# A planned one-core kernel (spectral filter, gated with a state-space scan): angle rounding in one ScalarE operation, four skip products on VectorE, single chunks at the end, joined products

## The chip, the cores and the metric

One core of one Trainium2 chip runs the whole kernel in one launch. Its engines work beside each other: TensorE (PE, matmuls into PSUM; its weight loads are a row of their own, PEld), VectorE (DVE), ScalarE (ACT), GpSimd (POOL, here almost only as issuer of accumulating transfers) and SyncE (SP, issuer of nearly all other transfers). The metric is the device time of one execution in microseconds; lower is better. Most executions of one kernel agree within 0.3%.

## What is computed

The input x has 2048 rows (sequence) and 1024 columns. Two branches are computed from it and mixed by a gate with one value per row:

```
x = A_x                                          # 1 x 2048 x 1024, bf16
g = sigmoid((x * gate_w).sum(-1, keepdims=True))
a = irfft2(rfft2(x) * (w_r + 1j * w_i))          # over rows and columns

dt = exp(log_dt); Lam_bar = exp(dt * Lam)        # 1024 complex states
Bu = x @ (((Lam_bar - 1) / Lam)[:, None] * B).T
h[t] = Lam_bar * h[t - 1] + Bu[t]                # 2048 steps
b = 2 * Re(h @ C.T) + x * Dskip
return g * a + (1 - g) * b
```

Both branches are given the same x.

## The kernel before, in words

**Spectral branch.** Both Fourier transforms are matmuls with constant cosine and sine tables. The row transform is split in two stages (16 x 128). Per step of 16: forward column transform (`fd`, L640), first row stage (`s1`, L663), a turn through DRAM, second row stage with the product by W on VectorE (`s2w`, L751; the product is L765, one operation for each of the two parts of W), first inverse stage (`is1`, L772), another turn through DRAM, second inverse stage and inverse column transform (`is2` L788, `idft` L804). Each result is moved out of PSUM by ScalarE. `idft` scales by the gate (L817) and writes half-folded rows to DRAM; `unfold` (L905) reads them back for two row tiles and adds and subtracts (L913, L917) into a buffer `ga`.

**State-space branch.** States are handled in eight blocks of 128 (`jb`), rows in four chunks of 512 (`c`). For a block, `bu` (L860) computes B x in PSUM (L870, 16 matmuls of 512 columns for a chunk), ScalarE moves it to `h` (L873), `rot` (L831) turns it by an angle that grows with the row, so that the scan on VectorE (L882) is a real one with one factor per state, and `rot_out` (L849) turns it back. A rotation is two products (L838, L839) and two sums (L840 and L842 or L844). It takes one chunk (n=1) or two (n=2). Before the change `bu` takes two chunks in each turn; `rot_out` takes chunks 0 and 1 singly and chunks 2 and 3 together. Blocks 6 and 7 come in the order (6, first half), (7, first half), (6, second half), (7, second half).

**Tables.** `table` (L610) makes cosine and sine for a block: the angle in turns is `tau * theta`; its nearest whole number is found by adding a large constant (L617, ScalarE, out in fp32) and taking it off again (L619, ScalarE), VectorE subtracts it (L620), ScalarE takes the sine of both parts (L622 to L624), casts them to bf16 singly (L625, L626), and scaled copies (L627, L628) feed the products with the input coefficients (L629, L632).

**Gates.** `gates` (L581): 32 matmuls with one output row each, sigmoid (L594), a cast to fp32 for each of four rows (L597), and a turn through DRAM into two layouts, `gA` (for L817) and `gB` (for 1 - g, `omg`).

**Output.** `yout` (L921), one row tile `tb` of 128 of the 16: 64 matmuls `h` x `C` of 512 columns (L929), in four groups `pc` of two state blocks, then the skip `x * Dskip` as eight matmuls of 128 columns with a diagonal matrix (L936). For tiles 0 to 11 ScalarE scales the result by 1 - g into two halves `y32` (L944), GpSimd issues transfers that add them onto `ga` (L945), and `ga` goes out (L947). For tiles 12 to 15 VectorE does it in one operation (L952) and SP sends `o` (L955); tile 15 in two halves.

**What sets the order.** Nothing is written in order of time. Each operation is entered in a `Plan` (L168) with an engine, a key, an assumed duration, and what it reads and writes. `Plan.run` (L236) goes through them once while the kernel is built: it takes the engine that can start soonest, and on it, among those that can start then, the operation with the lowest key. That fixes the order on every engine. The keys are linear in the block or tile number with the constants `K_...` (L386 to L428). Buffers are given from groups with few slots: four of PSUM (`ps`), two for `ga` and the transposed B (`bt`), eight in `cs` for tables, `y32` and `o`, five in `e4` for the unfold.

## Time and profile before

| what | us |
|---|---|
| median of 3 executions (lowest, highest) | 324.64 (324.59, 326.59) |
| the profiled execution, its own time | 325.01 |
| its span, first to last instruction | 323.2 |
| TensorE busy | 308.9 (96%) |
| VectorE busy | 285.2 (88%) |
| ScalarE busy | 204.6 (63%) |
| GpSimd busy | 22.5 (7%) |

All numbers of lines and groups are those of the profiled execution, whose time lies 1.81 us over its span. A row of a group of instructions reads: line, engine, operation, output and inputs, shapes, count, then busy time in us and mean ns of one, then the idle time of its engine just before and what ended it. Matmuls are pipelined, so the mean of one (379 ns at 512 columns) is longer than the spacing of two; spacings are read from the chain of work that ended last, whose pieces follow each other without gaps. The mean granted TensorE clock is 0.999.

### The profile page before, as it was taken

Reading aid. Unit: us, or ns where it says so; the run is one execution under the profiler, and the core shown is the slowest. Engines: PE = TensorE matmul, PEld = TensorE weight load, DVE = VectorE, ACT = ScalarE, POOL = GpSimd, SP = SyncE. Lnnn points to the kernel's source line nnn. Section 1 sums busy time; section 2 is a strip of 40 time slices with the busy share of each in tenths; the row PEclk is TensorE's granted clock in tenths of the full one; section 3 lists DMA queues with packets and bytes.
Section 4 is the critical chain, followed back from the end, with each engine's and each line's share of the span. In section 5 each row is a group of like instructions: output and inputs, shape, how many; then the busy total and the mean of one; then the engine's idle time right before and its main releaser. Section 6 shows DMA issues by size and latency. Waiting matters only on the chain.

```text
span 323.2 us, 5180 instructions
## 1 busy us (share of the span) xinstructions
PE 308.9 (96%) x1869; PEld 165.3 (51%) x1869; DVE 285.2 (88%) x448; ACT 204.6 (63%) x280; POOL 22.5 (7%) x32
## 2 busy tenths in 40 slices
PE   5988999999999999999988999999999999999994
PEld 4753666654444444444556655544544444454452
DVE  3999999999999999999899999999999999931114
ACT  3799999999899998999999998301411110050000
POOL 1000000000000000000000000000420242162000
PEclk9999999999999999999999999999999999999999
DMA  7996247795979999995699997970750368977003
GB/s 228 390 231 4 65 145 210 147 268 150 284 172 302 260 258 259 224 267 83 160 262 250 267 256 220 198 256 2 120 108 2 76 121 171 187 102 128 32 3 127
DMA packets 79408, 56.50 MB, mean 175 GB/s; under 512 B 49684, under 2 KB 65428, under 8 KB 79384
## 3 DMA queue, kind: packets, MB, share of 16 engines
q1 hardware_dynamic: 75848, 53.03, 63.5%
q0 software_dynamic: 3456, 3.15, 9.2%
q8 instruction: 14, 0.23, 0.3%
q14 instruction: 10, 0.08, 0.1%
q10 hardware_dynamic: 80, 0.01, 0.0%
HBM read 28.38 MB, written 16.79 MB: 140 GB/s over the span
## 4 chain that ended last, share of the span: by engine, by line
PE 62%; ACT 17%; DMA 9%; DVE 6%; issue 3%; SPq 2%; DVEq 0%; ACTq 0%
PE ps_y L929 34%; PE psu L870 14%; PE ps_id L812 2%; DMA wA<-in_A_w_r_dram 2%; PE ps_y L936 2%; ACT h L782 2%; ACT M_all L801 2%; PE ps_fd L648 2%; PE ps_fd L653 2%; PE ps_s L668 2%; DVE wA L765 1%; ACT h L873 1%; DMA Bcol<-turn_scratch 1%; DMA wB<-in_A_w_i_dram 1%; DMA xn<-in_A_x_dram 1%
## 5 line engine op out<-in xcount | busy, mean ns | idle before, releaser
L870 PE MATMUL psu<-xT,BTs 128*128 128x512 bf16 x512 | 116.7, 379 | 2.5 <-ACT M_all L513 1.1
L929 PE MATMUL ps_y<-CT,h 128*128 128x512 bf16 x512 | 113.6, 379 | 0.0
L870 PEld LDWEIGHTS <-BTs 128*128 128x128 bf16 x512 | 49.6, 98 | 61.0 <-issue 4.2
L929 PEld LDWEIGHTS <-h 128*128 128x128 bf16 x512 | 49.4, 98 | 56.0
L882 DVE TENSOR_TENSOR_SCAN h<-r_sb,carry,h 128x512 bf16<-128x512 f32 x48 | 60.0, 1272 | 0.0
L944 ACT ACTIVATE y<-ps_y,omg 128x512 f32<-128x512 f32 x24 | 15.3, 684 | 70.5 <-PE ps_y L936 60.8
L945 POOL DMA_DIRECT2D ga<-y x24 | 21.2, 1170 | 269.5 <-DVE h L840 225.5
L873 ACT CAST h<-psu 128x1024 bf16<-128x1024 f32 x32 | 32.4, 1022 | 3.0 <-PE psu L870 3.0
L840 DVE TENSOR_TENSOR h<-h,su 128x1024 bf16<-128x1024 bf16 (+1 forms) x40 | 23.0, 574 | 0.2
L839 DVE TENSOR_TENSOR h<-h,pn 128x1024 bf16<-128x1024 bf16 (+1 forms) x24 | 20.7, 861 | 0.1
L838 DVE TENSOR_TENSOR su<-h,pn 128x1024 bf16<-128x1024 bf16 (+1 forms) x24 | 20.6, 858 | 0.0
L839 DVE TENSOR_TENSOR h<-h,cs 128x2048 bf16<-128x2048 bf16 x16 | 19.5, 1221 | 0.2
L838 DVE TENSOR_TENSOR su<-h,cs 128x2048 bf16<-128x2048 bf16 x16 | 19.3, 1205 | 0.0
L882 DVE TENSOR_TENSOR_SCAN h<-r_sb,h 128x512 bf16<-128x512 f32 x16 | 18.8, 1208 | 0.0
L952 DVE SCALAR_TENSOR_TENSOR o<-ps_y,omg,ga 128x1024 bf16<-128x1024 f32 (+1 forms) x5 | 5.3, 1069 | 12.8 <-issue 11.0
L782 ACT CAST h<-ps_is 128x1024 bf16<-128x1024 f32 x16 | 16.0, 1017 | 0.4 <-PE ps_is L779 0.4
L917 DVE TENSOR_TENSOR ga<-G_all 128x512 bf16<-128x512 bf16 x16 | 5.9, 417 | 11.4 <-DMA out_dram<-ga 11.4
L762 ACT CAST h<-ps_s 128x1024 bf16<-128x1024 f32 x16 | 15.8, 1021 | 0.0
L478 PE MATMUL pt<-ident,xn 128*128 128x128 bf16 x128 | 10.1, 242 | 5.1 <-DMA xn<-in_A_x_dram 3.8
L817 ACT ACTIVATE M_all<-ps_id,gA 128x1024 bf16<-128x1024 f32 x12 | 13.6, 1162 | 1.0 <-PE ps_id L812 1.0
L801 ACT CAST M_all<-ps_is 128x1024 bf16<-128x1024 f32 x12 | 12.6, 1060 | 1.3 <-PE ps_is L797 1.3
L812 PE MATMUL ps_id<-G_all,M_all 128*128 128x256 bf16 x96 | 12.4, 273 | 0.8 <-ACT M_all L801 0.8
(135 smaller groups left out, 406.2 us busy)
## 6 DMA issues: line engine op xcount, KB each, us to landing
xn<-in_A_x_dram SPq DMA_DIRECT2D x16, 256.0 KB
h<-turn_scratch SPq DMA_DIRECT2D x16, 256.0 KB
turn_scratch<-h SPq DMA_DIRECT2D x16, 256.0 KB
M_all<-turn_scratch SPq DMA_DIRECT2D x13, 256.0 KB
ga_scratch<-M_all SPq DMA_DIRECT2D x12, 256.0 KB
M_all<-ga_scratch SPq DMA_DIRECT2D x6, 512.0 KB
ga<-y POOLq DMA_DIRECT2D x24, 128.0 KB, 5.0
out_dram<-ga SPq DMA_DIRECT2D x12, 256.0 KB
```

Of the source, the lines that this page charges most:

```text
L762: act(key, 1.01, lambda: nc.scalar.copy(out=X2.t, in_=ps2.t), r=[(ps2,)], w=[(X2,)])
L782: act(key, 1.01, lambda: nc.scalar.copy(out=C1.t, in_=psc.t), r=[(psc,)], w=[(C1,)])
L801: act(key, 1.01, lambda: nc.scalar.copy(out=ZT.t, in_=psz.t), r=[(psz,)], w=[(ZT,)])
L812: mm(pz.t[:, at, :], lhsT=ZT.t[:, 2 * par + half, c, :], rhs=Gi_sb[:, par, half, c, :], start=(half == 0), stop=(half == 1))
L838: dve(key, w, lambda: nc.vector.tensor_mul(out=sv(), in0=src()[:, ::-1], in1=bc(1)), r=sitem + [titem(1)], w=[(su,)])
L839: dve(key, w, lambda: nc.vector.tensor_mul(out=dst(), in0=src(), in1=bc(0)), r=sitem + [titem(0)], w=ditem)
L840: dve(key, h, lambda: nc.vector.tensor_add(out=dst()[:, 0], in0=dst()[:, 0], in1=sv()[:, 0]), r=[(su,)] + r0, w=r0)
L870: mm(psu.t[:, ri, :], lhsT=BT.t[:, ri, db, :], rhs=xT[c][:, db, :], start=(db == 0), stop=(db == 7))
L873: act(kb[cc] + K_KA, 1.01, lambda cc=cc, psu=psu: nc.scalar.copy(out=g()[:, :, cc, :], in_=psu.t), r=[(psu, 0), (psu, 1)], w=ui(cc) + ([(" ...
L882: dve(kd, 1.25, lambda cc=cc, ri=ri, carry=carry: nc.vector.tensor_tensor_scan(out=g()[:, ri, cc, :], data0=rb, data1=g()[:, ri, cc, :], i ...
L929: mm(psy.t[:, 512 * dh:512 * (dh + 1)], lhsT=hbuf[jb // 4].t[:, jb % 4, ri, P * tb:P * (tb + 1)], rhs=CT[pc].t[:, ri, jb % 2, 512 * dh:512 ...
L945: dma(key - 1, 1.3, lambda cols=cols, y32=y32: nc.gpsimd.dma_start(out=ga.t[:, tb % 2, cols], in_=y32.t, accum_op=ALU.add), r=[(y32,)] + [ ...
```

## The change

- `table`: L617 writes its product with `theta` straight as int32 (which rounds it), L619 is left out, the subtraction reads int32. The two casts to bf16 become one of both halves.
- `gates`: the rows stay bf16 on the way through DRAM; the four casts are left out, and one small ScalarE copy makes `gA` fp32.
- `s2w`: one VectorE product over both parts of W in place of two.
- `bu` takes a first chunk and a count. The second half of blocks 6 and 7 goes chunk by chunk, in the order (6, chunk 2), (7, chunk 2), (6, chunk 3), (7, chunk 3).
- `rot_out`: chunks 0 and 1 of blocks 0 to 5 together; those of blocks 6 and 7 singly as before; chunks 2 and 3 of these two singly.
- `yout`: tiles 12 to 15 have no skip matmuls. VectorE multiplies the tile's rows of x by a row of Dskip that was spread over the partitions by a transfer, and sums (1 - g) times that and `ga` into a new fp32 buffer `ro`; the last operation adds `ro`. Tile 15 is made and sent in pieces of 512, 256 and 256 columns. x, Dskip's row and `ro` take slots of the groups `cs` (up to four) and `e4` (up to four).
- All `K_...` constants have other values, and there are four new ones.

The diff, cut to its core:

```diff
-    g_dram = dram.tile([S], FP32, name="g_scratch")
+    g_dram = dram.tile([S], BF16, name="g_scratch")
...
-                 "Cq": ("m", 3), "ZT": ("m", 2), "eo": ("m", 3), "eoc": ("e4", 3), "pq": ("e4", 2)})
+                 "Cq": ("m", 3), "ZT": ("m", 2), "eo": ("m", 3), "eoc": ("e4", 3), "pq": ("e4", 2), "xs": ("cs", 4), "ro": ("e4", 4)})
...
-    K_UN = 3245.96
+    K_UN = 2287.79
-    K_R1 = -842.33
-    K_R2 = 2615.95
-    K_RS = 140.01
+    K_R1 = 1065.73
+    K_R2 = 5537.31
+    K_RS = 84.32
-    K_Y = -5745.79
-    K_YS = 508.42
+    K_Y = -5275.43
+    K_YS = 317.37
+    K_R3 = 1947.99
+    K_R4 = -1072.73
+    K_D3 = 1520.12
+    K_SK = -886.66
...
-        act(key, 0.72, lambda: A2(out=kk(), in_=tau_f, func=ACT.Identity, scale=at(thn), bias=MAGIC),
-            r=[("tau",), ("tht0",)], w=[(tt, 0)])
-        act(key, 0.63, lambda: A2(out=kk(), in_=kk(), func=ACT.Identity, bias=-MAGIC), r=[(tt, 0)], w=[(tt, 0)])
-        dve(key, 0.75, lambda: nc.vector.scalar_tensor_tensor(out=rr(), in0=tau_f, scalar=at(thn), in1=kk(), op0=ALU.mult,
+        act(key, 0.72, lambda: A2(out=kk().bitcast(I32), in_=tau_f, func=ACT.Copy, scale=at(thn)), r=[("tau",), ("tht0",)], w=[(tt, 0)])
+        dve(key, 0.75, lambda: nc.vector.scalar_tensor_tensor(out=rr(), in0=tau_f, scalar=at(thn), in1=kk().bitcast(I32), op0=ALU.mult,
...
-        act(key, 0.62, lambda: nc.scalar.copy(out=cs.t[:, 1, :], in_=sn_f()), r=[(tf, 0)], w=[(cs, 1)])
-        act(key, 0.62, lambda: nc.scalar.copy(out=cs.t[:, 0, :], in_=cs_f()), r=[(tf, 1)], w=[(cs, 0)])
+        act(key, 1.04, lambda: nc.scalar.copy(out=cs.t, in_=tf.t), r=[(tf, 0), (tf, 1)], w=[(cs, 0), (cs, 1)])
...
-            act(key, 0.6, lambda rr=rr: nc.scalar.copy(out=grow_f.t[rr, :], in_=grow.t[rr, :]), r=[(grow, c)], w=[(grow_f, c)])
...
+        act(key + 20, 0.22, lambda: nc.scalar.copy(out=gA, in_=gA_bf), r=[("gA_bf",)], w=[("gA",)])
...
-        for i in range(2):
-            dve(key + K_WD, 0.69, lambda i=i: nc.vector.tensor_mul(out=Z(b, i), in0=X2.t, in1=Z(b, i)),
-                r=[(X2,)], w=[wr + (i, c, o) for c, o in parts])
+        dve(key + K_WD, 1.22, lambda: nc.vector.tensor_mul(out=Zs(b), in0=X2.t[:, None, :, :].to_broadcast([P, 2, 2, K]), in1=Zs(b)),
+            r=[(X2,)], w=[wr + (i, c, o) for i in range(2) for c, o in parts])
...
+    dsk = tile_of([P, D], BF16, "dsk", "xs")
+    dma(K_UN - K_DM, 0.9, lambda: nc.sync.dma_start(out=dsk.t, in_=B_Dskip.rearrange("(o d) -> o d", o=1).to_broadcast([P, D])), r=[("step", 15, 1)], w=[(dsk,)])
...
-        order = [(pc, dh) for pc in range(4) for dh in range(2)] if tb < 15 else [(pc, dh) for dh in range(2) for pc in range(4)]
+        parts = [(0, 512), (512, 1024)] if tb < 15 else [(0, 512), (512, 768), (768, 1024)]
+        order = [(pc, v) for pc in range(4) for v in parts] if tb < 15 else [(pc, v) for v in parts for pc in range(4)]
...
+        if tb >= SKIP:
+            xs = tile_of([P, D], BF16, "xs", "xs")
+            dma(key - K_DM, 0.85, lambda: nc.sync.dma_start(out=xs.t, in_=x[P * tb:P * (tb + 1), :]), r=[("step", 15, 1)], w=[(xs,)])
+            ro = tile_of([P, D], FP32, "ro", "ro")
+            dve(key + K_SK, 0.69, lambda: nc.vector.tensor_mul(out=xs.t, in0=xs.t, in1=dsk.t), r=[(xs,), (dsk,)], w=[(xs,)])
+            dve(key + K_SK, 1.27, lambda: nc.vector.scalar_tensor_tensor(out=ro.t, in0=xs.t, scalar=og, in1=ga.t[:, tb % 2], op0=ALU.mult, op1=ALU.add),
+                r=[(xs,), ("omg",)] + ri_[0] + ri_[1], w=[(ro,)])
...
-    KD = lambda p: KB(p, 0) + K_D + K_KR * p + K_D1 * turns[p][1]
+    KD = lambda p, c0: KB(p, 0) + K_D + K_KR * p + K_D1 * (c0 > 0)
...
-    turns = [(jb, pr) for jb in range(6) for pr in range(2)] + [(6, 0), (7, 0), (6, 1), (7, 1)]
+    turns = [(jb, c0, 2, 2 * jb + c0 // 2) for jb in range(6) for c0 in (0, 2)]
+    turns += [(6, 0, 2, 12), (7, 0, 2, 13), (6, 2, 1, 14), (7, 2, 1, 14.5), (6, 3, 1, 15), (7, 3, 1, 15.5)]
...
+            if c0 == 0:
+                if jb < 6:
+                    rot_out(jb, 0, 2, KD(p, 0) + K_O)
+                else:
+                    rot_out(jb, 0, 1, KD(p, 0) + K_O)
+                    rot_out(jb, 1, 1, K_R1 + K_RS * jb)
             else:
-                rot_out(jb, 2, 2, K_R2 + K_RS * jb)
+                rot_out(jb, c0, n, (K_R2, K_R3)[c0 == 3] + K_RS * jb + K_R4 * (n == 1))
```

More of the change, by code (lines that the diff above doesn't have):

```diff
@@ L347, in tile_of @@
         if group == "e4":
-            return plan.buf(tag, lambda i: view(G_all[:, 2048 * (4 - i):2048 * (5 - i)] if i >= 3 else M_all[:, 2048 * i:2048 * (i + 1)], shape))
+            return plan.buf(tag, lambda i: view(G_all[:, 2048 * (4 - i):2048 * (5 - i)] if i >= 3 else M_all[:, 2048 * i:2048 * (i + 1)], shape, dtype))
         if group == "f":
@@ L575 @@
     sv(5, lambda: V.tensor_scalar_mul(out=ns2[:, :, 0], in0=sTC, scalar1=-1.0), ["sn2"], ["ns2a"])
-    gB, gA, omg = [cpool.tile([P, 16], FP32, name=n) for n in ("gB", "gA", "omg")]
-    omg_bf = cpool.tile([P, 16], BF16, name="omg_bf")
+    gA, omg = [cpool.tile([P, 16], FP32, name=n) for n in ("gA", "omg")]
+    gB, gA_bf, omg_bf = [cpool.tile([P, 16], BF16, name=n) for n in ("gB", "gA_bf", "omg_bf")]
     def gates(key):
@@ L943, in yout @@
                 y32 = tile_of([P, K], FP32, "y32", "cs")
-                act(key - 1, 0.72, lambda cols=cols, y32=y32: A2(out=y32.t, in_=psy.t[:, cols], func=ACT.Copy, scale=og), r=[(psy, dh), ("omg",)], w=[(y32,)])
+                act(key - 1, 0.72, lambda cols=cols, y32=y32: A2(out=y32.t, in_=psy.t[:, cols], func=ACT.Copy, scale=og), r=[(psy, 512 * dh), ("omg",)], w=[(y32,)])
                 dma(key - 1, 1.3, lambda cols=cols, y32=y32: nc.gpsimd.dma_start(out=ga.t[:, tb % 2, cols], in_=y32.t, accum_op=ALU.add),
```

148 lines of the change are left out of this document (76 added, 72 removed).

## The prediction, written before the result

> **What bounds the kernel now.** I read the page first: busy time and the 40 slices.
>
> ```profile
> PE 308.9 (96%) x1869; PEld 165.3 (51%) x1869; DVE 285.2 (88%) x448; ACT 204.6 (63%) x280; POOL 22.5 (7%) x32
> PE   5988999999999999999988999999999999999994
> DVE  3999999999999999999899999999999999931114
> ACT  3799999999899998999999998301411110050000
> ```
>
> TensorE is nearly always busy, VectorE until about 285 us, ScalarE until about 200 us. Averages hide which of them starves the others, so next came the windows of 20 us and TensorE's waits.
>
> ```profile
> 20.00:40.00 20.00, 18.87 (x101) 10.11 (x100) 19.74 (x29) 18.81 (x27) 0.00 (x0) 1.00 0.56 77
> 160.00:180.00 20.00, 18.10 (x162) 12.56 (x159) 19.97 (x33) 19.98 (x24) 0.00 (x0) 1.00 0.99 236
> 180.00:200.00 20.00, 19.22 (x147) 12.00 (x145) 19.86 (x30) 18.88 (x26) 0.00 (x0) 1.00 1.04 265
> 200.00:220.00 20.00, 20.00 (x112) 10.17 (x109) 19.98 (x33) 4.15 (x4) 0.00 (x0) 1.00 0.70 197
> 280.00:300.00 20.00, 20.00 (x118) 10.02 (x117) 6.17 (x14) 5.06 (x8) 6.99 (x8) 1.00 0.73 134
> ```
>
> ```profile
> PE psu L870 <- ACT M_all L513: 1.1, 1, 1.1
> PE ps_id L812 <- ACT G_all L801: 0.9, 2, 0.6
> PE ps_id L812 <- ACT M_all L801: 0.8, 1, 0.8
> PE psu L870 <- ACT G_all L817: 0.6, 1, 0.6
> PE psu L870 <- ACT M_all L817: 0.4, 1, 0.4
> ```
>
> The columns of a window are its length, then busy time of PE, weight loads, VectorE, ScalarE and GpSimd, the clock, the DMA share. From 200 us TensorE has no hole; the clock is 1.00. Its holes are: the first load of x, which nothing in the change touches, 1.1 us near 25 us, and 1.90 + 0.78 = 2.68 us between 160 and 200, where each wait is for a ScalarE eviction and ScalarE is busy 19.98 of 20. So time comes off in three places only: TensorE's own work, its waits for ScalarE, and what follows the last matmul. VectorE at 19.9 of 20 is busy beside TensorE, but TensorE does not wait for it.
>
> **The skip product leaves TensorE.** The chain at the end:
>
> ```profile
> 314.49 0.45 PE ps_y L936 x8
> 314.94 1.73 PE ps_y L929 x8
> 316.67 0.46 PE ps_y L936 x8
> 317.21 1.28 DVE o L952
> 318.53 0.75 DVE o L952
> 319.28 0.66 DVEq L1046
> ```
>
> ```profile
> 317.81 0.61 PE L936 MATMUL ps_y<-diag,xT 128*128 128x128 bf16 x8
> 47.97 0.44 PE ps_fd L648 x4
> ```
>
> Four tiles lose eight L936 matmuls each: 4 x 0.45 = 1.80 us, in a stretch where TensorE never waits. Tile 15's second half in two quarters turns 16 matmuls of 512 columns (1.73 / 8 = 0.216) into 32 of 256 (0.44 / 4 = 0.110): +0.06. Sum **-1.74**. A matmul of 128 columns costs 0.45 / 8 = 0.056 us here. The Trainium skill, page "TensorE: Matmul & The Clock Gate", section "Back-to-back issue gap", gives some 81 ns as the sustained spacing at 128 columns and 56 ns for an isolated one; by the 81 the 32 matmuls would be worth 2.6 us, an estimate from that page. The trace has 0.056 in a stream with weight loads, so I keep the row.
>
> **The end.** Tile 14's last matmul ends at 317.13; VectorE then adds tile 14 (1.28) and tile 15's halves and is done at 319.28 + 0.66 = 319.94; TensorE ends at 317.81 + 0.61 = 318.42, so 1.52 us of VectorE follow it, and 323.2 - 319.94 = 3.26 us of output DMA. New: after tile 14 TensorE has 0.86 (512 columns, one pc), 0.44 (256, one pc) and 0.88 (256, two) = 2.18 us left. VectorE's 1.28 covers the first; the pieces cost 0.75, 0.48 and 0.48 (1283 - 747 = 536 ns for 512 columns less, so 747 - 268), done 3.1 to 3.2 us after tile 14, some 1.0 behind TensorE in place of 1.52. **-0.5**. The last DMA has half the bytes; I count nothing for that (between 0 and -0.3, a tenth of its 3.26).
>
> **What VectorE gets in exchange, and the joins.**
>
> ```profile
> L838 DVE TENSOR_TENSOR su<-h,cs 128x2048 bf16<-128x2048 bf16 x16 | 19.3, 1205 | 0.0
> L840 DVE TENSOR_TENSOR h<-h,su 128x1024 bf16<-128x1024 bf16 x24 | 16.4, 684 | 0.2
> L840 DVE TENSOR_TENSOR h<-h,su 128x512 bf16<-128x512 bf16 x16 | 6.6, 410 | 0.0
> L765 DVE TENSOR_TENSOR wA<-h,wA 128x1024 bf16<-128x1024 bf16 x16 | 10.3, 689 | 0.1
> L952 DVE SCALAR_TENSOR_TENSOR o<-ps_y,omg,ga 128x1024 bf16<-128x1024 f32 x3 | 3.9, 1283 | 12.7 <-issue 11.0 <-PE ps_y L936 1.8
> L952 DVE SCALAR_TENSOR_TENSOR o<-ps_y,omg,ga 128x512 bf16<-128x512 f32 x2 | 1.4, 747 | 0.0
> ```
>
> Added: 4 x (0.69 + 1.28) = 7.9 us, the product by the 1024-wide row of L765, the fused sum by that of L952. W multiply joined: 16 x (1.21 - 2 x 0.689) = -2.7. Output rotation joined for chunks 0 and 1 of blocks 0 to 5: 2 x (2 x 0.69 + 2 x 0.41) = 4.4 becomes 2 x 1.21 + 2 x 0.68 = 3.8, six times: -3.6. The last two blocks' second half chunk by chunk: the same 0.6 back for two rotations in two blocks: +2.4. Net +4.0. It costs TensorE nothing: the sums need ga of tiles 12 to 15, so they fall into 285 to 312 us, where VectorE is idle (6.17 busy of 20 from 280 on; the 11.0 idle ahead of L952). The products can run earlier, in the full stretch, for 2.8 us, against 3.6 + 2.7 - 2.4 = 3.9 saved there. If that cover went, the next thing late would be tiles 8 to 11's last quarter at 282. The loads are 4 x 256 KB of x and 256 KB of Dskip on SP's queue, 1.25 of 56.5 MB, while the DMA engines are half empty; the Dskip load has no writer to wait for and can go out early, and x follows the last inverse step near 204 us, 90 us before its use.
>
> **What ScalarE loses.**
>
> ```profile
> L617 ACT ACTIVATE tt<-tau_f,tht 128x512 f32<-128x512 f32 x8 | 6.0, 746 | 0.5 <-DVE tht L550 0.5
> L619 ACT ACTIVATE tt<-tt 128x512 f32<-128x512 f32 x8 | 5.2, 649 | 0.1
> L625 ACT CAST cs<-tf 128x512 bf16<-128x512 f32 x8 | 5.1, 643 | 0.0
> L597 ACT CAST M_all<-M_all 1x512 f32<-1x512 bf16 x4 | 2.5, 616 | 0.1
> L467 DVE CAST tau_f<-tau_i 128x512 f32<-128x512 int32 x1 | 0.4, 426 | 0.0
> ```
>
> Per table: L619 goes (0.65), two copies of 0.64 become one of about 1.04: 0.9, eight times 7.1 us. Gates: four copies of 0.62 go, one small one (0.2) comes: 2.3. Together -9.4 of 204.6. The first operation of a table keeps L617's price, with int32 out; the VectorE operation that reads int32 is not in the trace, but L467 reads int32 at 0.43 us for 512, so I expect no loss; were it twice its 0.74, 6 us over eight tables would fall on VectorE, covered as above. Head: the table of block 0 stands in ScalarE's queue ahead of the eviction for which TensorE waits 1.1 us; L619 gone is 0.5 to 0.6 of it, I take **-0.4** (bounds: -1.1, the whole wait, and +0.5, another operation put there). 160 to 200 us: relief there is 2.3 of the gates just before it and 0.9 of the last table, 3.2 us, against 2.68 of waits. Not each eviction wait ends by relief elsewhere, and every priority is new. I take three quarters, **-2.0** (bounds: -2.7, and +1.9, a second hole like the worst window's).
>
> **Sum.** 323.2 - 1.74 - 0.5 - 0.4 - 2.0 = 318.56 us span; with the 325.01 - 323.2 = 1.81 around it, 320.4 for an execution like the profiled one. That one lies 0.37 over the median of 324.64, so the forecast is **320.0**, -1.4%.
>
> **Rivals.**
> First, only what leaves TensorE counts: the new priorities fill the ScalarE stretch otherwise and the holes stay. 323.2 - 2.24 = 320.96, **322.4** as a median. For it: ScalarE still stands at 195 of 323 us, nearly all before 200, so it stays as full there as the order lets it. Against: it is the releaser of every hole, and it has less to do.
> Second, all holes close: -1.74 - 0.5 - 1.1 - 2.7 - 0.3 gives 316.9, **318.3** as a median. Against: the plan balances three full engines.
> Third, slower: the slots for the scaled tiles run out.
>
> ```profile
> L944 ACT ACTIVATE y<-ps_y,omg 128x512 f32<-128x512 f32 x24 | 15.3, 684 | 70.5 <-PE ps_y L936 60.8 <-issue 6.1 <-DMA ga<-y 2.6
> 245.75 6.91 PE ps_y L929 x32
> 282.58 1.26 ACT L944 ACTIVATE y<-ps_y,omg 128x512 f32<-128x512 f32 x2 [20.82 <-PE ps_y L936]
> 289.91 1.26 ACT L944 ACTIVATE y<-ps_y,omg 128x512 f32<-128x512 f32 x2 [1.72 <-PE ps_y L936]
> 290.89 1.75 POOL L945 DMA_DIRECT2D ga<-y  x2 [1.24 <-ACT y L944]
> 300.47 1.43 DVE L917 TENSOR_TENSOR ga<-M_all 128x512 bf16<-128x512 bf16 x4 [2.93 <-DMA out_dram<-ga]
> DMA to landing us min/median/max: 3.0/5.0/6.8
> ```
>
> The y32 halves share eight buffers (group cs) with the tables, and now with Dskip's row and three tiles of x from about 205 us on. While the tables of blocks 6 and 7 also live, longer than now as chunk 3 comes last, two are left: one tile. A tile then takes 1.27 + 0.88 (half of 1.75) + 5.0 = 7.15 us through eviction, issue of its first half and landing of its second. TensorE brings one each 6.91 + 0.45 = 7.36, just slower. But tiles 8 to 11 finish together (282 to 290): the first would be evicted by 282.58 + 1.26 = 283.8 as now, the last by 283.8 + 3 x 7.15 = 305 in place of 289.91 + 1.26 = 291.2, its ga buffer, which tiles 14 and 15 wait for, would come 14 us later (314.3 in place of 300.47), and with 1.43, two sums, and 3.0 of final adds the span would be near 324.6. With landings of 6 us, between median and longest, it is 327.7 and **329** as a median, +1.4%. It decides from an eviction of tile 11 after about 307. Against: the unfolds of the early tiles now have lower keys than the rotations of chunks 2 and 3, which frees these buffers early, and the three other PSUM buffers take up 3 x 7.36 = 22 us.
> Fourth, the change does not do what it says: the joined operations cost what the parts did and the ScalarE holes move rather than shrink, with a new hole of the worst window's size (1.9): about **324.3**.
>
> **How the numbers follow.** Chances: forecast 0.52 (318.3 to 321.4), all holes 0.10, work alone 0.22, fourth 0.08, slots 0.08. Range: below, all holes and the last DMA's 0.3 with 0.4 of small ones, 317.6; above, the fourth, 324.3, which leaves out the slots and a little at each edge. A measurement of this kernel can tell about 1% from no change, 321.4 to 327.9: the forecast and all holes are faster (0.62, mostly just past the bound), work alone and the fourth no change (0.30), the slots slower (0.08).
>
> **What the profile after would show.** L936 96 matmuls in place of 128 and TensorE's end earlier by 1.7; VectorE's last add near 0.48 and 1.0 behind TensorE; ScalarE near 195 busy; TensorE's idle from 160 to 200 near 0.7; L620 with int32 near 744 ns; no TensorE wait for a y32 eviction after 200. Wrong would be shown by TensorE waits on L944, by L917's last four later than 305, by holes against VectorE in the middle, or by ScalarE idle in 160 to 200 while TensorE still waits.

## The result, and the profile after

| | before | after |
|---|---|---|
| median in one comparison, us (lowest to highest) | 325.29 (324.59 to 326.59) | 323.0 (322.9 to 323.8) |
| profiled execution: time, span | 325.01, 323.2 | 323.0, 321.2 |

The ratio is 0.9925, 95% interval 0.99 to 0.9951: 0.75% less (0.70% by the two medians), about half of the 1.4% that was forecast. The span of the profiled run fell by 2.0 us, where the prediction's sum was 4.64.

The engines of the kernel after, from its page:

```profile
PE 304.9 (95%) x1820; PEld 165.5 (52%) x1853; DVE 293.0 (91%) x433; ACT 197.0 (61%) x260; POOL 22.2 (7%) x32
```

VectorE is busy 7.8 us more than before (forecast: 4.0 more), ScalarE 7.6 us less (forecast: 9.4 less). TensorE's 4.0 less is no measure: 1820 matmuls stand beside 1853 weight loads, so 33 records are missing from this trace, about 0.1 us in each window of 20 us. Windows of the kernel after, columns as in the prediction:

```profile
20.00:40.00 20.00, 19.84 (x109) 10.71 (x110) 19.73 (x28) 16.71 (x22) 0.00 (x0) 1.00 0.71 90
40.00:60.00 20.00, 18.76 (x115) 12.38 (x117) 19.97 (x27) 19.88 (x23) 0.00 (x0) 1.00 0.47 139
60.00:80.00 20.00, 18.83 (x117) 11.28 (x118) 18.28 (x24) 18.33 (x23) 0.00 (x0) 1.00 0.98 231
160.00:180.00 20.00, 19.62 (x172) 13.79 (x172) 20.00 (x28) 18.38 (x22) 0.00 (x0) 1.00 1.00 227
180.00:200.00 20.00, 18.14 (x145) 12.12 (x146) 19.95 (x27) 15.80 (x17) 0.00 (x0) 1.00 1.08 248
```

The hole of 20 to 40 us is gone, new ones stand between 40 and 80, one of the two late windows is nearly full and the other emptier than before, while ScalarE is busy only 15.80 of 20 there: one of the signs by which the prediction said that it would be shown wrong. TensorE's idle from 160 to 200 us is 2.2 us, some 0.2 of it missing records; near 0.7 was forecast. Three of TensorE's waits in the kernel after, and two of other engines (us in total, times, longest):

```profile
ACT y L960 <- DMA ga<-y: 20.6, 11, 5.3
DVE ga L917 <- DMA out_dram<-ga: 1.8, 2, 1.1
PE ps_id L812 <- ACT M_all L801: 1.7, 1, 1.7
PE ps_y L933 <- DVE o L969: 1.4, 2, 0.8
PE ps_fd L649 <- ACT M_all L672: 0.6, 2, 0.3
```

The fourth row is new in kind: TensorE waits for VectorE's last operation. It stands at the very end, as the timeline of the kernel after shows (start, duration, instructions, idle before):

```profile
307.71 6.43 PE L933 MATMUL ps_y<-CT,h 128*128 128x512 bf16 x30
...
314.18 0.75 DVE L969 SCALAR_TENSOR_TENSOR o<-ps_y,omg,M_all 128x512 bf16<-128x512 f32 x1
314.99 0.60 PE L933 MATMUL ps_y<-CT,h 128*128 128x256 bf16 x4 [0.84 <-DVE o L969]
...
315.62 0.48 DVE L969 SCALAR_TENSOR_TENSOR o<-ps_y,omg,M_all 128x256 bf16<-128x256 f32 x1 [0.69 <-PE ps_y L933]
316.16 1.47 PE L933 MATMUL ps_y<-CT,h 128*128 128x256 bf16 x12 [0.57 <-DVE o L969]
...
317.67 0.48 DVE L969 SCALAR_TENSOR_TENSOR o<-ps_y,omg,M_all 128x256 bf16<-128x256 f32 x1 [1.56 <-PE ps_y L933]
```

From the last 512-column matmul (314.14) to TensorE's end (317.63) pass 3.49 us, for 16 matmuls of 256 columns. They write columns 768 to 1023 of tile 15, and begin only when VectorE has read columns 0 to 511 of it (314.93); the last twelve wait until it has read 512 to 767 (316.10). VectorE in its turn waits 0.69 us for the first four of them before it reads columns 512 to 767, which they do not write.

To compare kernels, the span is cut where TensorE does the same work in each: at the first transform matmul (L648, L649 after), at the first L812, and where the long stream of output matmuls begins behind the last L812. The rows of before, then of after:

```profile
36.68 0.60 PE L648 MATMUL ps_fd<-G_all,xpm 128*128 128x256 bf16 x4
...
163.03 1.05 PE L812 MATMUL ps_id<-G_all 128*128 128x256 bf16 x8 [0.63 <-ACT G_all L801]
...
204.06 6.21 PE L929 MATMUL ps_y<-CT,h 128*128 128x512 bf16 x28
```

```profile
37.12 1.04 PE L649 MATMUL ps_fd<-G_all,xpm 128*128 128x256 bf16 x8
...
163.37 1.04 PE L812 MATMUL ps_id<-G_all 128*128 128x256 bf16 x8
...
203.27 7.07 PE L933 MATMUL ps_y<-CT,h 128*128 128x512 bf16 x31
```

| us of the profiled run | start to A | A to B | B to C | C to TensorE's end | rest | span |
|---|---|---|---|---|---|---|
| before | 36.7 | 126.3 | 41.0 | 114.4 | 4.8 | 323.2 |
| after | 37.1 | 126.3 | 39.9 | 114.4 | 3.6 | 321.2 |
| own_tile | 36.9 | 125.6 | 39.9 | 113.8 | 3.5 | 319.7 |
| halves | 37.5 | 124.6 | 39.9 | 112.6 | 4.8 | 319.4 |
| halves_skip_on_pe | 37.0 | 125.9 | 39.9 | 114.4 | 4.2 | 321.3 |
| skip_back | 37.4 | 126.1 | 39.9 | 114.4 | 4.2 | 322.0 |
| old_keys | 37.5 | 129.3 | 42.9 | 111.8 | 3.6 | 325.1 |
| head_undone | 38.3 | 125.3 | 39.9 | 112.6 | 3.6 | 319.7 |
| late_undone | 37.2 | 129.6 | 40.3 | 112.6 | 3.6 | 323.3 |
| joins_undone | 37.7 | 125.4 | 39.9 | 113.3 | 3.6 | 319.9 |
| relief_old_order | 39.1 | 127.7 | 41.2 | 114.4 | 4.7 | 327.1 |
| tables_old_order | 38.4 | 126.6 | 41.2 | 114.4 | 4.7 | 325.2 |
| end_old_order | 36.8 | 126.4 | 41.0 | 120.0 | 3.5 | 327.7 |
| both_old_order | 37.0 | 129.5 | 41.2 | 119.9 | 3.6 | 331.3 |
| chunk_pairs | 37.9 | 124.6 | 39.9 | 121.9 | 3.6 | 328.0 |
| pairs_unfold_late | 37.5 | 125.5 | 39.9 | 119.4 | 3.6 | 325.8 |
| end_old_unfold_early | 38.0 | 126.3 | 41.1 | 113.7 | 3.7 | 322.8 |
| own_unfold_late | 37.1 | 125.7 | 39.9 | 112.6 | 3.6 | 318.9 |

Each row is one profiled execution. The first column depends on the first loads and varies by itself (36.8 and 38.0 in end_old_order and end_old_unfold_early, which do the same work up to there); the second varies by up to 1.7 (124.6 to 126.3 in kernels of the new order that differ only behind it). B to C repeats within 0.2 among kernels of one order (late_undone apart, where ScalarE has more to do). So does the fourth column where TensorE has no wait in it (112.6, or 114.4 with the skip product); own_tile and joins_undone have 113.8 and 113.3, as TensorE waits there for rotations of VectorE. The argument rests on these two columns. From before to after: B to C gave 1.1 us, the rest behind TensorE 1.2, and the fourth column, from which the skip product was to take 1.8, gave nothing. That makes 2.3; the profiled run of the kernel after began its transforms 0.4 us later and from A to B was level.

### The profile page after: what moved, and what is told of

Its sections match the earlier page's. It is cut to its first block, busy times and chain, and to the rows that moved or that the text cites. A ratio compares the mean times of both kernels' runs of the same rounds, so it can differ in the third digit from the quotient of the medians.

```text
span 321.2 us, 5066 instructions
## 1 busy us (share of the span) xinstructions
PE 304.9 (95%) x1820; PEld 165.5 (52%) x1853; DVE 293.0 (91%) x433; ACT 197.0 (61%) x260; POOL 22.2 (7%) x32
## 4 chain that ended last, share of the span: by engine, by line
PE 77%; ACT 10%; DVE 5%; issue 3%; DMA 2%; SPq 1%; DVEq 0%; ACTq 0%
PE ps_y L933 34%; PE psu L870 26%; PE ps_id L812 4%; DMA xn<-in_A_x_dram 2%; PE ps_is L797 2%; PE ps_is L778 2%; PE ps_y L941 2%; PE ps_is L779 2%; DVE h L882 1%; PE ps_fd L649 1%; PE ps_fd L654 1%; PE ps_s L760 1%; PE ps_s L669 1%; ACT M_all L672 1%; ACT M_all L660 1%
## 5 line engine op out<-in xcount | busy, mean ns | idle before, releaser
L870 PE MATMUL psu<-xT,BTs 128*128 128x512 bf16 x495 | 114.8, 379 | 2.6 <-ACT h L873 0.8
L933 PE MATMUL ps_y<-CT,h 128*128 128x512 bf16 (+1 forms) x515 | 112.1, 372 | 2.1 <-DVE o L969 1.4
L933 PEld LDWEIGHTS <-h 128*128 128x128 bf16 x528 | 51.1, 98 | 57.3 <-issue 1.8
L870 PEld LDWEIGHTS <-BTs 128*128 128x128 bf16 x512 | 49.7, 98 | 59.9 <-issue 3.3
L873 ACT CAST h<-psu 128x1024 bf16<-128x1024 f32 x32 | 32.5, 1023 | 4.7 <-PE psu L870 3.7
L839 DVE TENSOR_TENSOR h<-h,pn 128x2048 bf16<-128x2048 bf16 (+1 forms) x20 | 20.2, 1008 | 0.4
L838 DVE TENSOR_TENSOR su<-h,pn 128x2048 bf16<-128x2048 bf16 (+1 forms) x20 | 20.1, 1007 | 0.2
L839 DVE TENSOR_TENSOR h<-h,cs 128x2048 bf16<-128x2048 bf16 (+1 forms) x18 | 19.9, 1106 | 0.2
L838 DVE TENSOR_TENSOR su<-h,cs 128x2048 bf16<-128x2048 bf16 (+1 forms) x18 | 19.6, 1089 | 0.1
L817 ACT ACTIVATE M_all<-ps_id,gA 128x1024 bf16<-128x1024 f32 x14 | 15.2, 1118 | 3.4 <-PE ps_id L812 3.3
L763 ACT CAST h<-ps_s 128x1024 bf16<-128x1024 f32 x16 | 16.0, 1023 | 0.0
L660 ACT CAST M_all<-ps_fd 128x1024 bf16<-128x1024 f32 x13 | 13.8, 1091 | 0.0
L969 DVE SCALAR_TENSOR_TENSOR o<-ps_y,omg,G_all 128x1024 bf16<-128x1024 f32 x2 | 2.6, 1284 | 11.6 <-PE ps_y L933 11.6
L812 PE MATMUL ps_id<-G_all,M_all 128*128 128x256 bf16 x88 | 11.1, 273 | 1.7 <-ACT M_all L801 1.7
L801 ACT CAST M_all<-ps_is 128x1024 bf16<-128x1024 f32 x11 | 11.0, 1025 | 1.9 <-PE ps_is L797 1.9
```

The costliest lines, as they stand in the source:

```text
L660: act(key, 1.02, lambda: nc.scalar.copy(out=X1.t.rearrange("p c (n g r) -> p c n g r", g=2, r=2), in_=pf.t.rearrange("p r g c n -> p c n g ...
L763: act(key, 1.01, lambda: nc.scalar.copy(out=X2.t, in_=ps2.t), r=[(ps2,)], w=[(X2,)])
L812: mm(pz.t[:, at, :], lhsT=ZT.t[:, 2 * par + half, c, :], rhs=Gi_sb[:, par, half, c, :], start=(half == 0), stop=(half == 1))
L838: dve(key, w, lambda: nc.vector.tensor_mul(out=sv(), in0=src()[:, ::-1], in1=bc(1)), r=sitem + [titem(1)], w=[(su,)])
L839: dve(key, w, lambda: nc.vector.tensor_mul(out=dst(), in0=src(), in1=bc(0)), r=sitem + [titem(0)], w=ditem)
L870: mm(psu.t[:, ri, :], lhsT=BT.t[:, ri, db, :], rhs=xT[c][:, db, :], start=(db == 0), stop=(db == 7))
```

## Experiments

Each was timed against the kernel before on its own chip (medians of before: 324.91, 325.33, 325.53 and 325.81 us in the four sets). Ratios are to that kernel, with 95% intervals; they are not the quotients of the medians shown. Executions of one kernel spread by more than 0.3% here: the kernel before ran from 324.2 to 327.7 us in the largest set (23 executions).

**own_tile**: the kernel after, with the last 256 columns of tile 15 in a PSUM tile of their own; same order on every engine.

```diff
+        psq = psum([P, 256], "ps_q") if tb == 15 else None
...
-                        mm(psy.t[:, lo:hi], lhsT=hbuf[jb // 4].t[:, jb % 4, ri, P * tb:P * (tb + 1)],
+                        mm(psq.t if lo == 768 else psy.t[:, lo:hi], lhsT=hbuf[jb // 4].t[:, jb % 4, ri, P * tb:P * (tb + 1)],
```

> The changed kernel, with tile 15's last 256 columns in a PSUM tile of their own (a slot that tile 12 has left); the order on every engine is the same. Theory: TensorE waits twice at the end (0.84 and 0.57 us in its waits for L969) because those columns share a PSUM tile with columns that VectorE is reading. Then both waits go, the last matmul ends near 316.0 in place of 317.6, and the span falls from 321.2 by 1.4 to 1.7 us, to about 319.6; ratio to before about 0.988. Rival: the waits are for VectorE being behind with tile 14, whatever the tile: then the matmuls still stop, and the span stays within 0.3 us of 321.2.

321.29 us (320.18 to 322.92), ratio 0.9877 [0.9847, 0.9906]. The end in its timeline:

```profile
307.77 6.64 PE L934 MATMUL ps_y<-CT,h 128*128 128x512 bf16 x32
...
314.25 1.91 PE L934 MATMUL ps_q<-CT,h 128*128 128x256 bf16 x16
314.45 1.14 DVE L970 SCALAR_TENSOR_TENSOR o<-ps_y,omg,M_all 128x512 bf16<-128x512 f32 x2
316.19 0.48 DVE L970 SCALAR_TENSOR_TENSOR o<-ps_q,omg,M_all 128x256 bf16<-128x256 f32 x1 [0.60 <-PE ps_q L934]
```

The 16 matmuls follow without a wait: 1.75 us from the last 512-column one to TensorE's end in place of 3.49. In the profiles the shared tile cost 1.7 us; the ratio says 0.0048, 1.6 us, with intervals that touch (0.9906 and 0.99).

**halves** and **halves_skip_on_pe**: tile 15 in two halves again; the second also takes the four skip products back to TensorE.

```diff
-        parts = [(0, 512), (512, 1024)] if tb < 15 else [(0, 512), (512, 768), (768, 1024)]
+        parts = [(0, 512), (512, 1024)]
```

```diff
-SKIP = 12
+SKIP = 16
```

> The changed kernel with tile 15 in two halves as before the change, otherwise the same order. Theory (shared PSUM tile): TensorE does not wait at the end, but the last addition has 512 columns (0.75 us) in place of 256 (0.48) and comes after tile 14's and the first half's: VectorE ends some 1.2 us after TensorE in place of 0.5. Span 321.2 - 1.6 + 0.7 = about 320.3. If the split itself is what gains, the span is instead longer than 321.2, by the 0.3 to 0.7 us that the smaller last piece saves.

> The kernel of the run with two halves, and the skip products of tiles 12 to 15 back on TensorE as eight matmuls of 128 columns each; no product, no fp32 sum on VectorE, no loads of x and Dskip. Against that run, theory: TensorE never waits after 200 us, so its end moves by the matmuls alone, 4 x 0.45 = 1.8 us later; span about 322.1. Rival: the work that VectorE and the buffers no longer carry gives some of it back (up to 1 us), or the 32 matmuls cost more than their spacing (2.6 us by the rule of the page on TensorE): 322.9.

323.02 (321.17 to 323.92), 0.993 [0.9903, 0.9958], and 323.3 (322.97 to 323.75), 0.9937 [0.9914, 0.996]. In `halves` TensorE has no wait at the end either, and the span is 319.4 (expected: 320.3), which also speaks for the shared tile. The medians differ by 0.3, the profiled runs by 1.8 in the fourth column, of which 0.6 comes back behind TensorE. The spread of `halves` is too wide to price the skip, so it was tried again (skip_back).

**old_keys**: own_tile with every `K_` constant that the kernel before has; the four new ones stay.

```diff
-    K_UN = 2287.79
+    K_UN = 3245.96
...
-    K_F0 = 11.43
+    K_F0 = 225.83
```

> The kernel with the last quarter in its own PSUM tile, with the constants of before for every key that existed before; the edits all stand. Theory (the holes between 40 and 75 us come from the new order, not from the edits): with the old order of the transform stage TensorE's idle from 40 to 80 us falls from 2.4 to under 0.5, as in the kernel before, while the holes from 160 to 200 shrink below the 2.68 of before, since ScalarE has 7.6 us less to do. What the output stage does under the old keys is open; if it holds, the span is 1 to 2 us below that of the own-tile run, about 318. Rival (the edits make the holes, for instance the early load of Dskip or the longer joined operations): 40 to 80 stays near 2.4 idle.

327.51 (325.89 to 329.08), 1.0072 [1.005, 1.0094]: slower than before. TensorE is still idle 2.3 us between 40 and 80, so the constants alone do not make those holes. ScalarE's relief, the end and the joined product by W don't either: both_old_order, below, has all three in the kernel before's order and is idle 0.2 us there. What is left is the other edits (the joined output rotations among them) and the order that the planner makes with them. Without constants made for them the edits lose 3.7 us from A to B and 3.0 from B to C against own_tile.

**head_undone** and **late_undone**: own_tile with ScalarE's work put back, in the same place of the same order: tables 0 and 1 in the first, tables 2 to 7 and four copies of the gates in the second.

```diff
+        def turns_of_angle():
+            A2(out=kk(), in_=tau_f, func=ACT.Identity, scale=at(thn), bias=MAGIC)
+            return A2(out=kk(), in_=kk(), func=ACT.Identity, bias=-MAGIC)
...
+        def casts():
+            nc.scalar.copy(out=cs.t[:, 1, :], in_=sn_f())
+            return nc.scalar.copy(out=cs.t[:, 0, :], in_=cs_f())
```

> The kernel of own_tile with ScalarE's relief taken back for the tables of blocks 0 and 1 only: the rounding in two operations (746 and 649 ns) and two casts (643 ns each) in place of one of about 1.06 us, in the same place of the same order; every other engine's order is that of own_tile. ScalarE has 2 x 0.9 = 1.8 us more before 55 us. Theory (the head's gain is given back before 75 us, because VectorE, busy 19.7 to 19.9 of 20 between 20 and 40 us, decides when the transforms start): at most +0.3 us against own_tile's 321.29. Rival, the prediction's step for the head (ScalarE decides there): +0.4 to +1.1. Third: ScalarE sets the pace of the whole stretch from 20 to 75: the full +1.8.

> The kernel of own_tile with ScalarE's relief taken back for the tables of blocks 2 to 7 (6 x 0.9 = 5.4 us, from 59 to 147 us) and the gates (four more copies of one row of 512, 4 x 0.62 = 2.5 us, near 150), in the same places of the same order; the other engines' orders are those of own_tile. Theory (the 2.0 us that went from TensorE's holes between 160 and 200 came from ScalarE's relief): +2.0 us against own_tile's 321.29, to some 323.3, with TensorE idle 2.4 to 4 us between 160 and 200 in place of 1.97. Rival (the new order did it, the relief does not reach that far): 0 to +0.5 there. Third (ScalarE sets the pace all the way from 60 to 200): up to +7.9.

head_undone: 322.31 (321.49 to 322.89), 0.9892 [0.9862, 0.9923]; against own_tile 0.0015, 0.5 us, inside both intervals. late_undone: 326.28 (325.13 to 328.36), 1.0018 [0.9992, 1.0044]: 4.6 us more, and not where the theory put it: A to B 129.6 in place of 125.6, B to C only 40.3 in place of 39.9. TensorE's idle from 160 to 200 us is 4.7 in place of 1.97, but 2.0 of that is a wait from 160 to 162 us, ahead of B. That wait is for a read of PSUM by ScalarE with the gates' copies ahead of it in its queue; the other is the hole that all kernels of the new order have:

```profile
PE psu L884 <- ACT M_all L600: 2.0, 1, 2.0
PE ps_id L826 <- ACT M_all L815: 1.7, 1, 1.7
```

**joins_undone**: own_tile with two products by W in place of the joined one, same order.

```diff
+        def products():
+            for i in range(2):
+                last = nc.vector.tensor_mul(out=Z(b, i), in0=X2.t, in1=Z(b, i))
+            return last
```

> The kernel of own_tile with the joined spectrum product as two instructions again (16 x (2 x 0.69 - 1.22) = 2.6 us more on VectorE), in the same place of the same order on every engine. Theory, as the prediction had it (TensorE does not wait for VectorE, so its work costs nothing while some slack is left): within 0.3 us of own_tile's 321.29. Rival (VectorE, busy 19.9 of 20 from 40 to 220 us, sets the pace beside TensorE): +1.3 to +2.6, with TensorE waits on VectorE's products or on what stands behind them.

322.78 (321.66 to 323.38), 0.9908 [0.9878, 0.9939]: 0.0031 over own_tile, 1.0 us, with overlapping intervals, and no column of the profiled run from A on longer by more than 0.1. VectorE's busy time rose by 1.3 us (294.2 for 292.9), not by 2.6. Whether the time rose by nothing or by 1 us stays open.

**skip_back**: own_tile with the skip product on TensorE (`SKIP = 16`, without Dskip's row; tile 15's last two skip matmuls go to `ps_q`).

> The kernel of own_tile with the skip product of tiles 12 to 15 back on TensorE: 32 matmuls of 128 columns more, without Dskip's row, the four tiles of x, and VectorE's four products and four sums (7.9 us less on VectorE). Theory (TensorE is without a hole from 200 us on, so its matmuls count in full): 4 x 0.45 = +1.8 us against own_tile's 321.29, to 323.1. Rival (the halves pair differed by 0.3 us in the medians, because VectorE's extra work and its loads cost about as much in most runs as TensorE saves): +0.3 or less, and a smaller spread than own_tile's 2.7 us.

323.53 (322.04 to 325.08), 0.9929 [0.9899, 0.9959]: 0.0052 over own_tile, 1.7 us, with intervals that just overlap. The fourth column is 114.4, against 112.6 in the kernels of the new order with the skip on VectorE in which TensorE has no wait there: 1.8 us, the predicted 1.80.

**relief_old_order** and **tables_old_order**: the kernel before with ScalarE's relief alone, the order of all else unchanged; the second without the gates.

```diff
-        act(key, 0.63, lambda: A2(out=kk(), in_=kk(), func=ACT.Identity, bias=-MAGIC), r=[(tt, 0)], w=[(tt, 0)])
+        act(key, 0.63, lambda: None, r=[(tt, 0)], w=[(tt, 0)])
```

> The kernel before with ScalarE's relief alone, in the kernel before's own order on every engine: one rounding with int32 out, one cast of sine and cosine together, the gates in bf16 without their four copies (L617 to L626 and the gates; 9.4 us of ScalarE by the prediction's rows). Theory (late_undone: the relief is worth 3.6 us in the profiled run and more in the median; the new order gives part of it back between 40 and 80 us): 3.0 to 4.6 us less than before, a ratio of 0.986 to 0.991, TensorE idle 160 to 200 us under 1.0 in place of 2.68, and no new holes from 40 to 60. Rival (the prediction's size, 0.4 + 2.0): 2.4 less, 0.9926. Third (the relief pays only with an order made for it): 0 to 0.5 less.

> The kernel before with the tables' relief alone (one rounding with int32 out, one cast; 7.1 us of ScalarE), gates untouched, every order as before but for the missing ScalarE instructions. In relief_old_order a copy of the last gates stood at the head of ScalarE's queue and waited 3.5 us for its transfer, which the kernel after's order does not do. Theory (that wait alone made relief_old_order slower; relief pays in any order): 2 to 4 us less than before, a ratio of 0.988 to 0.994. Rival (in the old order the relief falls on places where ScalarE had slack, and the holes of 160 to 200 come from the order of the evictions): within 0.7 us of before, TensorE idle 160 to 200 still 2.0 to 3.0.

326.76 (325.88 to 328.87), 1.0043 [1.0024, 1.0062]. This is relief_old_order, slower than before. Its edit put the small copy of the gates at the head of ScalarE's queue, where it waited for its transfer:

```profile
ACT gA L604 <- DMA gA_bf<-g_scratch: 3.5, 1, 3.5
```

tables_old_order, without the gates: 325.63 (325.08 to 327.2), 0.9993 [0.9972, 1.0015]. Some 7 us less of ScalarE by its rows (4.4 in busy time) changed nothing, B to C is 41.2 against 41.0, and the late windows of tables_old_order look as in the kernel before, ScalarE full and TensorE idle 2.73:

```profile
160.00:180.00 20.00, 18.40 (x158) 12.41 (x156) 20.00 (x32) 19.98 (x24) 0.00 (x0) 1.00 1.02 233
180.00:200.00 20.00, 18.87 (x150) 12.39 (x148) 19.97 (x30) 19.64 (x27) 0.00 (x0) 1.00 1.09 257
```

**end_old_order** and **both_old_order**: the kernel before with the skip of four tiles on VectorE and the end of own_tile; the second also with relief_old_order's edits and the joined product by W.

```diff
+SKIP = 12
+    K_SK = -886.66
```

> The kernel before with the change of the end alone: skip product of tiles 12 to 15 on VectorE with its loads, tile 15 in three pieces with the last 256 columns in a PSUM tile of their own, the order of everything else that of the kernel before. Theory (the prediction's terms: 1.74 of TensorE and 0.5 behind it, both in full, since TensorE has no holes from 200 us on): 2.2 us less than before, a ratio of 0.993. Rival (the skip's loads and VectorE's 7.9 us cost about as much as they save in most runs): 0.5 to 0.9 less, 0.998.

> The kernel before with relief_old_order's and end_old_order's edits and the joined spectrum product (2.6 us less of VectorE), all in the kernel before's order: without the change's new priorities, the joined output rotations and the last blocks' chunks one by one. Theory (the places are different stretches, so the savings add, and the new order costs some 2 us between 40 and 80 us): 5 to 7 us less than before, a ratio of 0.979 to 0.985, faster than own_tile's 0.9877. Rival (the new order belongs to the gain: VectorE's added work falls on rotations that the old order had no room for): no better than own_tile, 0.988 or more.

330.81 (329.53 to 333.12), 1.0161 [1.0125, 1.0197], and 333.24 (333.03 to 334.44), 1.0238 [1.021, 1.0266]. Of the four expectations for the two only both_old_order's rival came true (no better than own_tile), and its reason was not shown. The waits of end_old_order:

```profile
ACT y L963 <- DMA ga<-y: 38.8, 13, 16.6
DVE ga L919 <- DMA out_dram<-ga: 12.2, 2, 10.8
PE ps_y L936 <- ACT y L963: 5.3, 1, 5.3
```

This is the prediction's third rival: the scaled tiles wait for their slots (38.8 us, 2.6 before), and TensorE waits 5.3 us for an eviction, from 267 to 272 us. The fourth column is 7.4 us over 112.6; the 2.1 us more go with a lower granted clock behind the wait (0.91 from 260 to 280 us). Why both_old_order takes 129.5 from A to B as well, where relief_old_order took 127.7, was not followed further.

**chunk_pairs**: own_tile with chunks 2 and 3 of the last two blocks together.

```diff
-    turns += [(6, 0, 2, 12), (7, 0, 2, 13), (6, 2, 1, 14), (7, 2, 1, 14.5), (6, 3, 1, 15), (7, 3, 1, 15.5)]
+    turns += [(6, 0, 2, 12), (7, 0, 2, 13), (6, 2, 2, 14), (7, 2, 2, 15)]
```

> The kernel of own_tile with chunks 2 and 3 of the last two blocks rotated together again, as the kernel before has them (2.4 us less of VectorE); the order is own_tile's up to 235 us or so. Theory (VectorE has work enough in hand there, so the size of its pieces decides little): within 0.5 us of own_tile's ratio of 0.9877. Rival A (VectorE is full until 285 us and its rotations are what TensorE's last tiles wait for): 1 to 2.4 us less, 0.980 to 0.985. Rival B (the pieces let tiles 8 to 11 start earlier): 1 us more or worse, 0.991.

329.18 (327.24 to 331.34), 1.0109 [1.0068, 1.0149]: 7.5 us more by the ratio, with VectorE doing less. Its waits:

```profile
PE ps_y L934 <- DVE h L840: 5.5, 1, 5.5
PE ps_y L934 <- DVE h L842: 1.1, 1, 1.1
```

The fourth column is longer by more than these 6.6 us, 121.9 against 112.6. Behind the long wait TensorE ran at a lower granted clock, 0.83 from 280 to 300 us; ten matmuls of 512 columns took 4.62 us, where elsewhere eight take 1.89:

```profile
280.00:300.00 20.00, 14.51 (x81) 6.88 (x80) 6.28 (x7) 5.01 (x8) 6.07 (x7) 0.83 0.34 45
285.87 4.62 PE L934 MATMUL ps_y<-CT,h 128*128 128x512 bf16 x10 [5.49 <-DVE h L840]
```

**pairs_unfold_late**, **end_old_unfold_early** and **own_unfold_late** move only the unfolds: later in chunk_pairs, earlier in end_old_order, later in own_tile.

```diff
-            ga = unfold(tb, K_UN + K_YS * tb)
+            ga = unfold(tb, K_UN + 1600 + K_YS * tb)
```

```diff
-            ga = unfold(tb, K_UN + K_YS * tb)
+            ga = unfold(tb, 2287.79 + K_YS * tb)
```

> The kernel of chunk_pairs (329.2 us, ratio 1.0109) with the unfold operations at a lower priority, so that they stand behind more of VectorE's rotations; the orders of TensorE, ScalarE and GpSimd are those of chunk_pairs. Theory (TensorE's 5.5 us wait for a rotation at 280 to 286 us came from some 8 us of unfolds and their wait for an output, which stood ahead of the joined rotations): the rotations end at about 280, the hole goes, 4 to 6 us less, a ratio of 0.993 to 0.998. Rival (with later unfolds the eight y32 buffers run out instead, as in end_old_order, where TensorE waited 5.3 us for an eviction): no better than 1.009, with the wait on ScalarE's scaled tiles in the place of the wait on the rotation.

> The kernel of end_old_order (330.8 us, ratio 1.0161) with the unfolds' priority of the kernel after (earlier by some 960), chunks of the last blocks still in pairs. Theory (the 5.3 us in which TensorE waited for an eviction came from y32 buffers held by tiles whose unfold came late): that wait falls under 1.5 us. Whether the time falls with it is what the run tells: theory A, it does, to 326 or less (1.002); theory B (as in chunk_pairs, the early unfolds push VectorE's joined rotations back): TensorE waits for rotations in its place, 3 to 6 us, and the time stays over 328 (1.008).

> The kernel of own_tile with the unfolds at a lower priority (later by some 1600 of the planner's units), chunks one by one as in own_tile. Theory (the unfold that waits 2.2 us for an output at 246 us, with the rotations behind it, costs TensorE 0.8 us in some runs and makes the spread): 0.5 to 1 us less than own_tile's 0.9877 and a spread under 2 us. Rival (later unfolds hold the y32 buffers longer and TensorE waits for evictions): 1 to 4 us more, 0.991 to 1.000.

pairs_unfold_late: 327.47 (324.8 to 328.63), 1.0038 [1.0013, 1.0063], 2.3 us less by the ratio, where 4 to 6 were expected. The wait for the rotation falls from 5.5 to 3.6 us and stays where it was:

```profile
PE ps_y L934 <- DVE h L840: 3.6, 1, 3.6
```

The unfolds were only a part of it. That a joined rotation is done later than the single chunk that tiles 8 to 11 need would explain the rest; no run shows it apart. end_old_unfold_early: 323.24 (322.85 to 324.53), 0.9919 [0.9889, 0.9949], 7.9 us less by the ratio for one constant. The wait for the eviction shrinks from 5.3 to

```profile
PE ps_y L936 <- ACT y L963: 0.9, 1, 0.9
```

so that wait did hang on the unfolds (ScalarE still waits 34.8 us for slots, 38.8 in end_old_order, but nearly all of it without TensorE), and chunk pairs do no harm in that order. It is the change of the end with the unfolds earlier, 2.6 us faster than before by the ratio (forecast for the end's two terms: 2.24); earlier unfolds without the change of the end were not run. own_unfold_late: 320.77 (320.29 to 322.47), 0.9857 [0.9824, 0.9889], the fastest of all; from own_tile it can't be told apart with certainty, and its spread is 2.2 us. In own_tile an unfold waits for an output with rotations behind it, and TensorE waits for those later,

```profile
248.23 1.43 DVE L917 TENSOR_TENSOR ga<-M_all 128x512 bf16<-128x512 bf16 x4 [2.16 <-DMA out_dram<-ga]
```

```profile
265.86 0.39 PE L934 MATMUL ps_y<-CT,h 128*128 128x512 bf16 x1 [0.59 <-DVE h L840]
```

and in own_unfold_late the window of 260 to 280 has no hole (fourth column 112.6 in place of 113.8).

## Where the prediction was right and where it failed

Two steps failed: that TensorE's last matmuls are free of VectorE, which cost the 1.74 us of the skip product, and that ScalarE's relief closes the holes of 160 to 200 us. The measured 323.0 lies near the first rival's 322.4, but by luck: that rival kept the holes and lost nothing at the end.

**The skip product, 1.74: right in size, and hidden.** skip_back and the fourth column give 1.8; the medians of the halves pair, with the widest spread, give 0.3. The trace's 0.056 us for a matmul of 128 columns held; by the sustained 81 ns that the Trainium skill gives (page "TensorE: Matmul & The Clock Gate", section "Back-to-back issue gap") 2.6 us would have come, an estimate from that page; skip_back's 1.8 does not agree with it. But the cover that it was said not to need was at the end itself, below.

**The end, 0.5: this step failed.** "VectorE's 1.28 covers the first; the pieces cost 0.75, 0.48 and 0.48" took TensorE's last matmuls to be free of VectorE. They write the tile that VectorE is reading, and 1.7 us of waiting took back all that the skip had given. It also misread the order: all 16 matmuls of the last quarter come behind tile 15's first half, 1.76 us, not 0.88. That helps VectorE, whose last piece ends 0.52 us behind TensorE (318.15 against 317.63) where 1.0 was forecast; what follows TensorE fell by 1.2, not 0.5. With the wait removed and the unfolds later the two terms are worth 3.0 us of span (114.4 + 4.8 before, 112.6 + 3.6 in own_unfold_late) in place of 2.24. The ratio of that kernel is 0.9857, and 320.0 / 324.64 = 0.9857 was forecast. This is luck: it is another kernel, its interval is 0.9824 to 0.9889, and it gains more at the end and less in the holes.

The Trainium skill, page "PSUM — Partial Sum Buffer", section "PSUM bank collisions raise a hardware error", says that a compiler back end adds a dependency between instructions of two engines that touch the same bank in the same quarter of the partitions; the page gives a bank 2 KiB in each partition. By that the wait for columns 512 to 767 was to be foreseen (same 512 fp32 as the last 256), the one for columns 0 to 511, 0.84 us, was not; the trace has both. own_tile shows that a tile of its own takes both away; what puts the first one there was not tried.

**The holes of 160 to 200, 2.0: half the size, and for the wrong reason.** The same work, B to C, takes 1.1 us less. The step "relief there is 2.3 of the gates just before it and 0.9 of the last table" is wrong: relief in the old order gives 41.2 for 41.0, the new order without the late relief 40.3. The order shortens this stretch, while TensorE's idle from 160 to 200 us is still 2.0 in own_tile and own_unfold_late (2.68 before, near 0.7 forecast). The relief pays by letting the new order stand: without it A to B takes 4 us more (2.0 of that the wait behind the gates' copies, just ahead of B; where the other 2 come from was not followed). The hole that remains is the wait of 1.7 us for L801, which is in every profile of the new order shown here; in own_unfold_late that eviction stands in ScalarE's queue behind one (191.7 us) that has waited 0.60 us for its own matmuls, and less work elsewhere doesn't shorten that.

**The head, 0.4: nothing to be seen.** The 1.1 us hole is gone and taking the relief back there (head_undone) costs 0.5 us, inside both intervals; the transforms begin at 36.9 to 38.3 us in kernels of the new order and 36.7 to 39.1 of the old one, and VectorE is busy 19.7 of 20 there in both. In the gap TensorE does one group of eight L870 matmuls early (88 in place of 80 before A in before and own_tile), which it then lacks between 40 and 80: A to B has 1.73 us less work in own_tile and is 0.8 shorter. The waits for L672 (0.32 us, three times) account for the remainder in size.

**Joins and added VectorE work: single prices right, the net wrong, the cover right only in one order.** In the kernel after:

```profile
L621 ACT ACTIVATE tt<-tau_f,tht 128x512 int32<-128x512 f32 x8 | 6.1, 762 | 0.8 <-DMA xn<-in_A_x_dram 0.6 <-DVE pn L633 0.3
L622 DVE SCALAR_TENSOR_TENSOR tt<-tau_f,tht,tt 128x512 f32<-128x512 f32 x8 | 5.9, 742 | 0.0
L627 ACT CAST cs<-tf 128x1024 bf16<-128x1024 f32 x8 | 8.6, 1076 | 0.0
L765 DVE TENSOR_TENSOR wA<-h,wA 128x2048 bf16<-128x2048 bf16 x8 | 9.4, 1225 | 0.0
L951 DVE TENSOR_TENSOR xs<-xs,dsk 128x1024 bf16<-128x1024 bf16 x4 | 2.7, 683 | 0.0
L952 DVE SCALAR_TENSOR_TENSOR M_all<-xs,omg,ga 128x1024 f32<-128x1024 bf16 x2 | 2.6, 1282 | 0.0
```

The skip's 7.9 us came as forecast. The 3.9 us that the joins were to save did not show in busy time: skip_back, which has the joins and not the skip, is busy 285.3 us on VectorE, the kernel before 285.2. The forecast multiplied mean durations. Operations that follow each other overlap a little: the 32 products by W of before were busy 20.6 us together, at a mean of 0.688 each (22.0), and the joined 16 are busy 18.9, so 1.7 was saved there and not 2.7. "It costs TensorE nothing" holds in own_unfold_late. With rotations in pairs TensorE waited 3.6 to 6.6 us for them, and with late unfolds in the old order 5.3 us for an eviction.

**The third rival** was right as a mechanism and didn't happen here. The reason given against it fits: in end_old_unfold_early the unfolds' lower keys took TensorE's wait from 5.3 to 0.9 us. In the kernel after the wait on the slots grew from 2.6 to 20.6 us without reaching TensorE.

## What to carry to other kernels

Before splitting a last tile so that one engine finishes it in pieces, look whether the pieces still lie in one buffer that another engine writes: here the split paid only once the last piece had a tile of its own. Relief of an engine need have no price of its own while other things fix its order (here nothing for the tables in the old order, 4.6 us for tables 2 to 7 and the gates in the new one); price it by the stretch whose work is the same in both kernels, and expect it to pay through the order that it permits. An edit tested alone in an order made for other edits can lose more (here 5 us for one that gains 2.6) than it is worth: move one key before dropping it.

## What the runs showed of the hardware

Rounding by an int32 output cost ScalarE what the fp32 output did: 746 ns in tables_old_order and 762 in the kernel after, against 746 before. VectorE read int32 at no loss (742 ns against 744 in the kernel before). Two casts of 512 columns joined into one took 1076 ns (1058 in tables_old_order) against 643 + 634.

A long wait of TensorE can cost more than itself: behind waits of 3.6, 5.3 and 5.5 us (pairs_unfold_late, end_old_order, chunk_pairs) the mean granted clock of the window fell to 0.83, 0.91 and 0.83. The wait of 2.0 us in late_undone left it at 1.00.
